# The last dispatch laid out anew, a third late place for weights, and w2 of three experts by columns

## The chip, the cores and the metric

The kernel runs on one core of a Trainium2 chip. A core has a matrix engine (TensorE; PE in the profile, its weight loads PEld), three engines for elementwise work (VectorE, ScalarE and GpSimd; DVE, ACT and POOL), a sync engine (SyncE, SP) from whose queue most transfers start, and 16 DMA engines between HBM and on-chip memory. The metric is the device time of one execution in microseconds (us). Before and after are compared by the median of their runs.

## The reference

```python
x = attention(rmsnorm(q) * g_q, rmsnorm(k) * g_k, v)   # 4 x 12 heads x 448 x 64 -> 1792 x 768
x = relu(x @ w_in) ** 2 @ w_out                        # 768 -> 2048 -> 768
logits = x @ phi                                       # 1792 x 32: 8 experts, 4 slots each
d = softmax(logits, axis=0);  slot_input = d.T @ x     # dispatch: over all 1792 tokens
h = relu(slot_input[e] @ w1[e]);  slot_out[e] = h @ w2[e]      # for each expert e
out = softmax(logits, axis=1) @ slot_out               # combine: over the 32 slots
```

The data are fp32. The weights w1 and w2 of the eight experts are 25 MB each.

## The kernel before, in words

One batch is 448 tokens and 12 heads. Attention goes through 24 pairs of heads. Beside it runs a filler (`Fill`), a list of generators: after a batch's last pair, `moe_hidden(b)` for that batch is appended, and attention gives it a turn according to costs written by hand (`PACE`, and the numbers that `yield` gives back). The last batch's `moe_hidden` runs when attention is over. The framework puts each engine's instructions into a fixed order when the program is built, by what it expects to be ready, and adds the semaphores; on the chip each engine follows its order.

`moe_hidden(b)` computes 16 blocks of 128 hidden units (`fc`): 18 matmuls (`ph`), relu on ScalarE, square on another engine (`gt`, 128 x 448). The hidden activations are not multiplied by w_out token by token. w_out @ phi is made beforehand (`wp`), so logits come straight from `gt`; and the dispatch sums `gt` over tokens first, and multiplies the 32 sums by w_out after. `group(g)`, for four blocks each: four matmuls give partial logits, one 32-row strip of a PSUM bank for each block, which VectorE adds to `lsb` (L567); then 16 transposes and four copies make `gn`, the same four blocks with tokens on partitions.

`dispatch(b)`: one matmul with `r4` adds the four strips of `lsb` and repeats the sum in each (L633); VectorE takes the maximum (`nmx`), ScalarE the exponential (`et`), four transposes and a copy give `en` (L656). For each group four matmuls weight `gn` by `en`, and VectorE adds the result to the running sums `gacc` (L664). At the end the combine softmax over slots is made from `lsb` (L668 to L680). After the last batch's dispatch, 16 matmuls with `i4s` add the strips of `gacc`, divide by the softmax sum and turn the result round (`gtt`, L821 to L825). Then `si_ps` = `gtt` times w_out (L850), then for each expert w1 (`pe`), relu into `hpad`, and w2 (`so_ps`); `finish` adds `so_ps`'s strips, splits the result in two parts (`stt`), multiplies by the combine weights `ct`, and sends the output.

[...] `si_ps` takes the two banks that `mps()` had.

Weights come in pieces of 128 x 1536 (768 KB) into 25 places (L795): 18 once attention's memory is free, two once the last `whl` tile is (`ring3`), five once `moe` is (`ring2`). The list `todo` fixes the order: 14 pieces of w_in, 8 of w_out (`wo`), 32 of w1, 32 of w2. A place is loaded again as soon as `done(key)` says that its piece was used, so each `fetch` on SyncE's queue waits for the matmuls of an older piece. For the last NL = 2 experts, w2 is cut by columns: two pieces hold three chunks each of columns 0 to 511 (2 KB runs in HBM), one has two full chunks, and a fourth has columns 512 to 767 of six chunks (1 KB runs). These fourth pieces come last of all, and `finish(0, 512)` doesn't need them:

```python
    for e in range(E):
        for x in range(3 if e >= E - NL else 4):
            expert_out(e, x)
    finish(0, CA)
    for e in range(E - NL, E):
        expert_out(e, 3)
    finish(CA, DM)
```

Of the kernel before, what the change touches and what calls it, by code (L numbers as in the profile page):

```python
# [47 lines left out]
def tile_attention_moe_softmoe(  # L48
# [49 lines left out]
    sel4 = const.tile([128, 2, 64], F32R, tag="sel4", name="sel4")  # L98
# [79 lines left out]

    xf = {}
# [363 lines left out]
    def moe_hidden(b):  # L543
# [12 lines left out]

        def group(g):
# [3 lines left out]
            ps = mps()  # L561
            for fi in range(4):
                mm(ps[32 * fi : 32 * fi + 32, :S], wp[:, 4 * g + fi, :], gt[fi])
            if g == 0:
                nc.vector.tensor_copy(lsb, ps[:, :S])
            else:
                nc.vector.tensor_tensor(lsb, lsb, ps[:, :S], ALU.add)  # L567
            yield 0.8
# [15 lines left out]
        pend = None  # L584
        for fc in range(NFC):
# [6 lines left out]
            for kc in range(KC):  # L592
# [3 lines left out]
                if kc % 3 == 2:  # L596
                    yield 1.7
            if n < LATE:
                w_load(n + 2)
            else:  # L600
                done(("wi", fc, 0))
# [18 lines left out]
            if b == B - 1:  # L620
                state["fc"] += 1
        for c in pend:
            yield c
# [3 lines left out]
        if b == B - 1:  # L627
            state["fc"] += 1
        yield from dispatch(b, lsb, gn)

    def dispatch(b, lsb, gn):
        ps = mps()
        mm(ps[:, :S], r4.rearrange("p j s -> p (j s)"), lsb)  # L633
# [3 lines left out]
        et = keep.tile([128, S], F32, tag="et", name=f"et_{b}", bufs=1)  # L637
        nc.vector.tensor_reduce(nmx, ps[:, :S], AX.X, ALU.max)
        if b > 0:
            nc.vector.tensor_tensor(nmx, nmx, m_run, ALU.max)  # L640
            nc.vector.tensor_tensor(al, m_run, nmx, ALU.subtract)
            nc.scalar.activation(al, al, AF.Exp)
        nc.vector.tensor_copy(m_run, nmx)
        nc.vector.tensor_scalar(nmx, nmx, -1.0, None, ALU.mult)
        nc.scalar.activation(et, ps[:, :S], AF.Exp, bias=nmx)
# [5 lines left out]
        yield 0.8  # L651
        ps = mps()
        for c in range(NC):
            nc.tensor.transpose(ps[:CP, c * NS : (c + 1) * NS], et[:NS, c * CP : (c + 1) * CP], ident[:NS, :NS])
        en = keep.tile([CP, NC, NS], F32, tag="en", name=f"en_{b}", bufs=1)
        nc.vector.tensor_copy(en, ps[:CP, : NC * NS].rearrange("p (c s) -> p c s", c=NC))  # L656
        yield 0.4
        for g in range(NG):
            ps = mps()
            for c in range(NC):  # L660
                mm(ps[32 * c : 32 * c + 32, :], en[:, c, :], gn[g][:, c, :])
            gs = gacc[g // 2][:, (g % 2) * 512 : (g % 2 + 1) * 512]
            if b > 0:
                nc.vector.scalar_tensor_tensor(gs, gs, al, ps, ALU.mult, ALU.add)  # L664
            else:
                nc.vector.tensor_copy(gs, ps)
            yield 0.9
        ps = mps()  # L668
        for c in range(NC):
            mm(ps[:CP, c * NS : (c + 1) * NS], lsb[:, c * CP : (c + 1) * CP], i4)  # L670
        pc = ps[:CP, : NC * NS].rearrange("p (c s) -> p c s", c=NC)
# [8 lines left out]
        nc.vector.tensor_tensor(cb, cb, cm[:, :, None].broadcast_to([CP, NC, NS]), ALU.mult)  # L680
        yield 0.8
# [48 lines left out]
    NL = 2  # L730
# [64 lines left out]
    SLOTS, SLOTS2, SLOTS3 = 18, 5, 2  # L795
# [15 lines left out]
    for _ in range(SLOTS2):  # L811
        fetch(ring2, SLOTS2)
    while fill.step() is not None:
        pass
    ex = tc.alloc_tile_pool(name="ex", bufs=1)
    srv = ex.tile([128, 1], F32, tag="srv", name="srv")
    nc.vector.tensor_scalar(srv, s_run, TINY, None, ALU.add)
    nc.vector.reciprocal(srv, srv)
# [202 lines left out]
```

## Time and profile before

| | |
|---|---|
| runs, median (lowest to highest) | 872.99 us (871.06 to 875.35) |
| profiled execution, its own time | 878.86 us |
| its span, first to last instruction | 877.10 us |
| TensorE busy | 755.5 us |
| VectorE, ScalarE, GpSimd busy | 557.8, 440.9, 133.9 us |
[...]
| bytes moved | 185.25 MB |

The rows below are from the profiled execution; their times count from its first instruction. A busy time is the union of an engine's instructions. One fp32 matmul stands as two records, so four matmuls are eight records.

### The profile page before, as it was taken

How to read it: one execution, taken by the hardware profiler on the slowest of the kernel's cores; microseconds unless marked ns; L12 is line 12 of the kernel's file. 1: busy time of each engine (PE TensorE's matmuls, PEld its weight loads, DVE VectorE, ACT ScalarE, POOL GpSimd, SP SyncE). 2: the span in 40 equal slices, each digit the busy share in tenths (PEclk: the TensorE clock that was granted, in tenths of full speed). 3: DMA queues.
4: the chain of work that ended last, by engine and by line, in shares of the span. 5: the costliest groups of instructions: out<-in, count | busy, mean ns of one | idle time of the engine just before them, and what ended most of it. 6: DMA issues, size and time to landing. Idle time of an engine off the chain costs nothing.

```text
span 877.1 us, 11761 instructions
## 1 busy us (share of the span) xinstructions
PE 755.5 (86%) x4040; PEld 532.6 (61%) x4040; DVE 557.8 (64%) x1030; ACT 440.9 (50%) x711; POOL 133.9 (15%) x132
## 2 busy tenths in 40 slices
PE   0497768879999999999999999999989998988563
PEld 0254445556678787768778766787877885534011
DVE  6795758888889786988777878866535123220013
ACT  2584746777778566746546665555442122010002
POOL 4140120220222121213122121211010000000000
PEclk9997877968999999999999999999999998799996
DMA  9795666787575554325435343433438996599978
GB/s 254 248 295 182 216 202 195 216 254 227 193 222 196 168 183 121 113 73 167 147 111 172 115 135 95 125 115 96 144 102 322 415 396 213 237 415 415 414 286 252
DMA packets 72988, 185.25 MB, mean 211 GB/s; under 512 B 17408, under 2 KB 41440, under 8 KB 72928
## 3 DMA queue, kind: packets, MB, share of 16 engines
q1 hardware_dynamic: 66736, 159.10, 52.6%
q0 software_dynamic: 5632, 25.17, 9.4%
q8 instruction: 32, 0.52, 0.3%
q10 hardware_dynamic: 560, 0.23, 0.1%
q14 instruction: 28, 0.23, 0.1%
HBM read 148.73 MB, written 24.38 MB: 197 GB/s over the span
## 4 chain that ended last, share of the span: by engine, by line
PE 64%; DMA 12%; DVE 11%; ACT 8%; issue 3%; SPq 1%; ACTq 0%; DVEq 0%
PE ph L138 25%; PE pss L138 11%; PE pv L138 10%; PE pm L138 7%; DMA w<-in_moe_w_dram 5%; PE pm L576 3%; DMA m<-m 3%; PE pe L138 3%; ACT p L338 2%; DMA wi_s<-wf 2%; ACT ph L342 2%; DVE pl L343 1%; DVE nm L316 1%; PE pt L138 1%; DVE wf L462 1%
## 5 line engine op out<-in xcount | busy, mean ns | idle before, releaser
L138 PE MATMUL ph<-xh,whl 128*128 128x448 f32 x900 | 217.4, 375 | 5.4 <-ACT gt L603 2.6
L138 PEld LDWEIGHTS ph<-xh,whl 128*128 128x128 f32 x900 | 165.5, 188 | 30.5 <-ACT gt L603 5.7
L138 PE MATMUL pss<-m,s 65*112 65x448 f32 (+1 forms) x384 | 119.3, 423 | 13.2 <-DMA m<-mt 7.5
L338 ACT ACTIVATE p<-pss 112x896 f32<-112x896 f32 x96 | 87.9, 917 | 49.9 <-PE pss L138 49.2
L316 DVE TENSOR_REDUCE nm<-pss 112x2 f32<-112x896 f32 x96 | 102.6, 1087 | 15.5 <-PE pss L138 14.2
L138 PEld LDWEIGHTS pss<-m,s 65*112 65x112 f32 (+1 forms) x384 | 72.5, 193 | 38.4 <-issue 18.5
L343 DVE TENSOR_TENSOR pl<-p,ph 112x896 fp32r<-112x896 f32 x62 | 71.4, 1153 | 31.7 <-ACT ph L342 31.4
L138 PE MATMUL pss<-s,m 128*112 128x448 f32 x192 | 62.5, 420 | 27.4 <-DMA m<-m 23.3
L138 PE MATMUL pv<-ph,vst 112*65 112x448 f32 (+1 forms) x272 | 82.5, 379 | 0.1
L252 POOL TENSOR_TENSOR qs<-qk,y 112x512 f32<-112x512 f32 x48 | 59.4, 1248 | 152.0 <-issue 58.0
L603 ACT ACTIVATE gt<-ph 128x448 f32<-128x448 f32 x64 | 34.8, 543 | 93.3 <-PE ph L138 86.2
L138 PE MATMUL pv<-p,vf 112*65 112x448 f32 x112 | 61.2, 661 | 5.6 <-ACT p L338 4.6
L611 POOL TENSOR_TENSOR gt<-gt 128x448 f32<-128x448 f32 x33 | 35.3, 1070 | 193.0 <-ACT gt L603 193.0
L342 ACT ACTIVATE ph<-pss 112x896 fp32r<-112x896 f32 x68 | 62.3, 916 | 0.1
L138 PEld LDWEIGHTS pss<-s,m 128*112 128x112 f32 x192 | 33.7, 191 | 46.5 <-issue 13.3
L138 PE MATMUL ph<-xh,wi 128*128 128x448 f32 x252 | 53.3, 367 | 0.0
L364 ACT COPY t<-pv 65x448 f32<-65x448 f32 x48 | 25.3, 527 | 53.9 <-PE pv L138 53.9
L138 PE MATMUL pv<-pl,vst 112*65 112x448 f32 x136 | 50.4, 370 | 1.8 <-DVE pl L343 1.8
L138 PEld LDWEIGHTS ph<-xh,wi 128*128 128x128 f32 x252 | 46.6, 188 | 3.4
L611 DVE TENSOR_TENSOR gt<-gt 128x448 f32<-128x448 f32 x22 | 13.7, 623 | 53.1 <-ACT gt L603 53.0
L138 PEld LDWEIGHTS pv<-ph,vst 112*65 112x65 f32 (+1 forms) x272 | 35.1, 136 | 16.9 <-ACT ph L342 1.9
L138 PE MATMUL so_ps<-w,hpad 128*32 128x512 f32 (+1 forms) x256 | 32.0, 493 | 15.4 <-DMA w<-in_moe_w_dram 15.4
(144 smaller groups left out, 1144.1 us busy)
## 6 DMA issues: line engine op xcount, KB each, us to landing
w<-in_moe_w_dram SPq DMA_DIRECT2D x62, 768.0 KB
whl<-wi_s SPq DMA_DIRECT2D x50, 768.0 KB
w<-in_moe_w_out_dram POOLq DMA_DIRECT2D x16, 768.0 KB, 5.6
w<-in_moe_w_in_dram POOLq DMA_DIRECT2D x16, 768.0 KB, 7.7
wi<-wi_s SPq DMA_DIRECT2D x14, 768.0 KB
wi_s<-wh SPq DMA_DIRECT2D x16, 384.0 KB
wi_s<-wf SPq DMA_DIRECT2D x16, 384.0 KB
wo_s<-wf SPq DMA_DIRECT2D x16, 384.0 KB
```

Of the source, the lines that this page charges most:

```text
L138: nc.tensor.matmul(o, lhsT, rhs, start=start, stop=stop)
L252: nc.gpsimd.tensor_tensor(x.rearrange("p c h d -> p h c d"), live[t]["qk"][i], y[:, 8 * i : 8 * i + 8] .rearrange("p (h c) -> p h c", h=2) ...
L316: nc.vector.tensor_reduce(nm[:, 2 * half : 2 * half + 2], ps[:CP, :, :S], AX.X, ALU.max, negate=True)
L338: nc.scalar.activation(p, ps[:CP, :, :S], AF.Exp)
L342: nc.scalar.activation(ph, ps[:CP, :, :S], AF.Exp)
L343: engine(ON_PL[t // NP * 4 + 2 * j + half]).tensor_tensor(pl, p, raw(ph), ALU.subtract)
L364: nc.scalar.copy(tt[: D + 1, j, :], ps[: D + 1, :S])
L462: nc.vector.scalar_tensor_tensor(fi, lo, 29, fi, ALU.logical_shift_right, ALU.bitwise_or)
L576: nc.tensor.transpose(ps[:CP, fi * 128 : (fi + 1) * 128], gt[fi][:, c * CP : (c + 1) * CP], ident)
L603: nc.scalar.activation(gt, ps[:, :S], AF.Relu)
L611: (nc.vector if k else nc.gpsimd).tensor_tensor(gt, gt, gt, ALU.mult)
```

## The change

In the last batch the partial logits of blocks 12 to 14 and the `r4` matmul are made inside block 15 (`partial`), the latter in a bank `lg` that stays open; block 15's logits are added into that bank by four matmuls, one for each strip. The maximum and the exponential (`peak`) read `lg` and come ahead of group 3's transposes. `et` overwrites `lsb`. In `dispatch_last` the `i4s` matmuls of a group follow the weighting of the next one, with a ScalarE copy for each group, and the combine softmax comes last, from transposes of `lg`. For the other batches, `et` becomes one of the six `gt` buffers. Everywhere the maximum is taken negated, and `en` is copied ahead of the sum over `et`. `ring3` has three places, and NL is 3, so w2 of experts 5 to 7 is cut by columns. `finish` subtracts the part that ScalarE wrote, so one VectorE copy is gone. `sel4`, `et` and `ch` move in memory.

```diff
-    sel4 = const.tile([128, 2, 64], F32R, tag="sel4", name="sel4")
...
+    sel4 = att.tile([128, 2, 64], F32R, tag="sel4", name="sel4")
...
+        last = b == B - 1
+        lg = []
+        def partial():
+            ps = mps()
+            for fi in range(3):
+                mm(ps[32 * fi : 32 * fi + 32, :S], wp[:, NFC - 4 + fi, :], gts[NFC - 4 + fi])
+            nc.vector.tensor_tensor(lsb[:96], lsb[:96], ps[:96, :S], ALU.add)
+            yield 0.8
+            lg.append(hps())
+            mm(lg[0][:, :S], r4.rearrange("p j s -> p (j s)"), lsb, True, False)
+            yield 0.8
...
         def group(g):
             gt = gts[4 * g : 4 * g + 4]
-            ps = mps()
-            for fi in range(4):
-                mm(ps[32 * fi : 32 * fi + 32, :S], wp[:, 4 * g + fi, :], gt[fi])
-            if g == 0:
-                nc.vector.tensor_copy(lsb, ps[:, :S])
+            if last and g == NG - 1:
+                for j in range(4):
+                    mm(lg[0][32 * j : 32 * j + 32, :S], wp[:, NFC - 1, :], gt[3], False, True)
+                yield 0.8
             else:
-                nc.vector.tensor_tensor(lsb, lsb, ps[:, :S], ALU.add)
-            yield 0.8
+                ps = mps()
+                for fi in range(4):
+                    mm(ps[32 * fi : 32 * fi + 32, :S], wp[:, 4 * g + fi, :], gt[fi])
+                if g == 0:
+                    nc.vector.tensor_copy(lsb, ps[:, :S])
+                else:
+                    nc.vector.tensor_tensor(lsb, lsb, ps[:, :S], ALU.add)
+                yield 0.8
...
+        first = partial()
         for fc in range(NFC):
...
                 if kc % 3 == 2:
                     yield 1.7
+                    if last and fc == NFC - 1:
+                        yield next(first)
...
+        if last:
+            yield next(pend)
+            nmx, al, sb = peak(b, lg[0], lsb)
         for c in pend:
             yield c
...
-        if b == B - 1:
+        if last:
             state["fc"] += 1
-        yield from dispatch(b, lsb, gn)
+            yield 0
+            yield from dispatch_last(lg[0], lsb, gn, al, sb)
+        else:
+            yield from dispatch(b, lsb, gn)
...
+    def peak(b, ps, et):
         nmx = keep.tile([128, 1], F32, tag="nmx", name=f"nmx_{b}", bufs=2)
         al = keep.tile([128, 1], F32, tag="al", name=f"al_{b}", bufs=2)
         sb = keep.tile([128, 1], F32, tag="sb", name=f"sb_{b}", bufs=2)
-        et = keep.tile([128, S], F32, tag="et", name=f"et_{b}", bufs=1)
-        nc.vector.tensor_reduce(nmx, ps[:, :S], AX.X, ALU.max)
+        nc.vector.tensor_reduce(nmx, ps[:, :S], AX.X, ALU.max, negate=True)
         if b > 0:
-            nc.vector.tensor_tensor(nmx, nmx, m_run, ALU.max)
-            nc.vector.tensor_tensor(al, m_run, nmx, ALU.subtract)
+            nc.vector.tensor_tensor(nmx, nmx, m_run, ALU.min)
+        nc.scalar.activation(et, ps[:, :S], AF.Exp, bias=nmx)
+        if b > 0:
+            nc.vector.tensor_tensor(al, nmx, m_run, ALU.subtract)
             nc.scalar.activation(al, al, AF.Exp)
         nc.vector.tensor_copy(m_run, nmx)
-        nc.vector.tensor_scalar(nmx, nmx, -1.0, None, ALU.mult)
-        nc.scalar.activation(et, ps[:, :S], AF.Exp, bias=nmx)
+        return nmx, al, sb
+
+    def slots(b, et, al, sb):
+        ps = mps()
+        for c in range(NC):
+            nc.tensor.transpose(ps[:CP, c * NS : (c + 1) * NS], et[:NS, c * CP : (c + 1) * CP], ident[:NS, :NS])
+        en = keep.tile([CP, NC, NS], F32, tag="en", name=f"en_{b}", bufs=1)
+        nc.vector.tensor_copy(en, ps[:CP, : NC * NS].rearrange("p (c s) -> p c s", c=NC))
         if b > 0:
             nc.vector.tensor_reduce(sb, et, AX.X, ALU.add)
             nc.vector.scalar_tensor_tensor(s_run, s_run, al, sb, ALU.mult, ALU.add)
         else:
             nc.vector.tensor_reduce(s_run, et, AX.X, ALU.add)
-        yield 0.8
-        ps = mps()
+        return en
+
+    def weighted(b, g, ps, en, gn, al):
         for c in range(NC):
-            nc.tensor.transpose(ps[:CP, c * NS : (c + 1) * NS], et[:NS, c * CP : (c + 1) * CP], ident[:NS, :NS])
-        en = keep.tile([CP, NC, NS], F32, tag="en", name=f"en_{b}", bufs=1)
-        nc.vector.tensor_copy(en, ps[:CP, : NC * NS].rearrange("p (c s) -> p c s", c=NC))
-        yield 0.4
-        for g in range(NG):
-            ps = mps()
-            for c in range(NC):
-                mm(ps[32 * c : 32 * c + 32, :], en[:, c, :], gn[g][:, c, :])
-            gs = gacc[g // 2][:, (g % 2) * 512 : (g % 2 + 1) * 512]
-            if b > 0:
-                nc.vector.scalar_tensor_tensor(gs, gs, al, ps, ALU.mult, ALU.add)
-            else:
-                nc.vector.tensor_copy(gs, ps)
-            yield 0.9
-        ps = mps()
-        for c in range(NC):
-            mm(ps[:CP, c * NS : (c + 1) * NS], lsb[:, c * CP : (c + 1) * CP], i4)
-        pc = ps[:CP, : NC * NS].rearrange("p (c s) -> p c s", c=NC)
+            mm(ps[32 * c : 32 * c + 32, :], en[:, c, :], gn[g][:, c, :])
+        gs = gacc[g // 2][:, (g % 2) * 512 : (g % 2 + 1) * 512]
+        if b > 0:
+            nc.vector.scalar_tensor_tensor(gs, gs, al, ps, ALU.mult, ALU.add)
+        else:
+            nc.vector.tensor_copy(gs, ps)
+
+    def combine_softmax(b, pc):
         cm = keep.tile([CP, NC], F32, tag="cm", name=f"cm_{b}", bufs=1)
         cb = cnat[:, b]
...
+    def dispatch(b, lsb, gn):
+        ps = mps()
+        mm(ps[:, :S], r4.rearrange("p j s -> p (j s)"), lsb)
+        et = moe.tile([128, S], F32, tag="gt", name=f"et_{b}", bufs=6)
+        nmx, al, sb = peak(b, ps, et)
+        yield 0.8
+        en = slots(b, et, al, sb)
+        yield 0.4
+        for g in range(NG):
+            weighted(b, g, mps(), en, gn, al)
+            yield 0.9
+        ps = mps()
+        for c in range(NC):
+            mm(ps[:CP, c * NS : (c + 1) * NS], lsb[:, c * CP : (c + 1) * CP], i4)
+        combine_softmax(b, ps[:CP, : NC * NS].rearrange("p (c s) -> p c s", c=NC))
+        yield 0.8
+
+    def dispatch_last(lg, et, gn, al, sb):
+        b = B - 1
+        en = slots(b, et, al, sb)
+        srv = state["ex"].tile([128, 1], F32, tag="srv", name="srv")
+        nc.vector.tensor_scalar(srv, s_run, TINY, None, ALU.add)
+        nc.vector.reciprocal(srv, srv)
+        i4s = state["ex"].tile([128, 32], F32, tag="i4s", name="i4s")
+        nc.vector.tensor_scalar(i4s, i4, srv, None, ALU.mult)
+        yield 0.4
+        gps = hps()
+        for g in range(NG + 1):
+            if g < NG:
+                weighted(b, g, mps(), en, gn, al)
+            if g > 0:
+                for fc in range(4 * g - 4, 4 * g):
+                    fo = fc % 8 * 128
+                    mm(gps[:, fc * NS : (fc + 1) * NS], gacc[fc // 8][:, fo : fo + 128], i4s)
+                f4 = slice(4 * g - 4, 4 * g)
+                nc.scalar.copy(gtt[:, f4], gps.rearrange("p (f s) -> p f s", s=NS)[:, f4])
+            yield 0.9
+        lgs = et[:NS]
+        nc.scalar.copy(lgs, lg[:NS, :S])
+        ps = mps()
+        for c in range(NC):
+            nc.tensor.transpose(ps[:CP, c * NS : (c + 1) * NS], lgs[:, c * CP : (c + 1) * CP], ident[:NS, :NS])
+        combine_softmax(b, ps[:CP, : NC * NS].rearrange("p (c s) -> p c s", c=NC))
...
-    NL = 2
+    NL = 3
...
-    SLOTS, SLOTS2, SLOTS3 = 18, 5, 2
+    SLOTS, SLOTS2, SLOTS3 = 18, 5, 3
...
     for _ in range(SLOTS2):
         fetch(ring2, SLOTS2)
+    ex = tc.alloc_tile_pool(name="ex", bufs=1)
+    state["ex"] = ex
     while fill.step() is not None:
         pass
-    ex = tc.alloc_tile_pool(name="ex", bufs=1)
-    srv = ex.tile([128, 1], F32, tag="srv", name="srv")
-    nc.vector.tensor_scalar(srv, s_run, TINY, None, ALU.add)
-    nc.vector.reciprocal(srv, srv)
-    i4s = ex.tile([128, 32], F32, tag="i4s", name="i4s")
-    nc.vector.tensor_scalar(i4s, i4, srv, None, ALU.mult)
-    ps = hps()
-    for fc in range(NFC):
-        fo = fc % 8 * 128
-        mm(ps[:, fc * NS : (fc + 1) * NS], gacc[fc // 8][:, fo : fo + 128], i4s)
-    nc.vector.tensor_copy(gtt, ps.rearrange("p (f s) -> p f s", s=NS))
...
-        ch = keep.tile([128, S], F32, tag="et", name=f"ch_{b}", bufs=1)
+        ch = keep.tile([128, S], F32, tag="lsb", name=f"ch_{b}", bufs=1)
...
         st = stt[:96, c0:c1]
-        sth = stt[:, DM + c0 : DM + c1]
         nc.vector.tensor_copy(sos, so_ps[:, c0:c1])
         ps = tps()
         mm(ps[:, :w], r4.rearrange("p j s -> p (j s)"), sos)
         nc.scalar.copy(st[0:64], ps[0:64, :w])
-        nc.vector.tensor_copy(sth[64:96], ps[64:96, :w])
-        nc.vector.tensor_tensor(st[64:96], ps[64:96, :w], raw(sth[64:96]), ALU.subtract)
+        nc.vector.tensor_tensor(st[64:96], ps[64:96, :w], raw(st[0:32]), ALU.subtract)
```

## Rows read from the trace of the kernel before

**Rows 1.** Stretches: length, busy us of each engine (xinstructions), PEclk, DMA share, GB/s.
```profile
672.00:720.00 48.00, 47.99 (x268) 41.64 (x264) 11.41 (x22) 10.27 (x20) 0.00 (x0) 1.00 1.02 415
720.00:739.20 19.20, 18.47 (x104) 13.88 (x96) 4.95 (x8) 5.31 (x10) 0.00 (x0) 1.00 0.56 184
749.60:758.40 8.80, 8.02 (x52) 6.15 (x55) 2.29 (x10) 0.71 (x3) 0.00 (x0) 0.59 0.01 5
758.40:847.00 88.60, 66.75 (x556) 24.40 (x548) 7.21 (x15) 5.90 (x19) 0.00 (x0) 0.98 1.02 407
847.00:850.30 3.30, 2.17 (x9) 0.77 (x10) 0.69 (x1) 0.00 (x0) 0.00 (x0) 1.00 0.87 279
850.30:855.60 5.30, 4.52 (x29) 1.75 (x30) 2.67 (x4) 1.74 (x4) 0.00 (x0) 1.00 0.02 6
855.60:874.50 18.90, 6.96 (x33) 4.20 (x29) 7.77 (x13) 5.75 (x11) 0.00 (x0) 0.72 0.97 290
```

**Rows 2.** The chain that ended last: start, length, work.
```profile
742.28 7.22 PE pm L138 x40
749.50 5.24 PE ph L138 x32
755.50 8.31 PE si_ps L138 x48
...
847.26 1.95 PE so_ps L138 x4
```

**Rows 3.** SyncE's queue, 745 to 765 us: what its issues waited for.
```profile
SPq L764 <- PE si_ps L138: 19.6, 6, 16.3
```

**Rows 4.** Timeline of TensorE from the last hidden block: start, length, work.
```profile
733.33 0.95 PE L138 MATMUL pm<-gt,wp 128*32 128x448 f32 x6
734.69 0.94 PE L138 MATMUL pm<-gt,wp 128*32 128x448 f32 x2
737.67 0.65 PE L576 MATMUL pm<-ident,gt 128*112 128x128 f32 x4 [0.24 <-ACT gn L148]
738.16 1.02 PE L138 MATMUL pm<-lsb,r 128*128 128x448 f32 x2
741.32 0.58 PE L654 MATMUL pm<-ident,et 32*112 32x32 f32 x4 [2.15 <-ACT et L645]
```

**Rows 5.** Timeline of VectorE and ScalarE, same stretch and just behind.
```profile
734.01 0.62 DVE L611 TENSOR_TENSOR gt<-gt 128x448 f32<-128x448 f32 x1 [2.97 <-ACT gt L603]
739.21 0.63 DVE L638 TENSOR_REDUCE nmx<-pm 128x1 f32<-128x448 f32 x1 [0.16 <-PE pm L138]
740.63 0.63 ACT L645 ACTIVATE et<-pm,nmx 128x448 f32<-128x448 f32 x1 [0.17 <-DVE nmx L644]
741.93 0.29 DVE L656 COPY en<-pm 112x128 f32<-112x128 f32 x1
749.88 0.28 DVE L675 TENSOR_TENSOR w<-pm,cm 112x128 f32<-112x128 f32 x1
```

**Rows 6.** Stretches of the dispatch, columns as in rows 1.
```profile
733.40:740.80 7.40, 5.07 (x26) 2.19 (x26) 3.19 (x8) 2.57 (x6) 0.00 (x0) 1.00 0.51 150
742.20:747.60 5.40, 5.32 (x28) 1.29 (x32) 2.20 (x7) 0.00 (x0) 1.81 (x1) 0.50 1.01 419
749.30:751.10 1.80, 1.80 (x19) 1.80 (x18) 0.75 (x4) 0.71 (x3) 0.00 (x0) 1.00 0.14 55
751.20:754.80 3.60, 3.52 (x17) 3.39 (x16) 0.04 (x1) 0.00 (x0) 0.00 (x0) 0.50 0.00 0
```

**Rows 7.** Stretches of the last weight transfers, columns as in rows 1.
```profile
825.50:831.50 6.00, 3.27 (x28) 0.58 (x32) 0.00 (x0) 0.00 (x0) 0.00 (x0) 1.00 1.02 417
832.50:845.00 12.50, 7.18 (x42) 1.32 (x42) 0.00 (x0) 0.00 (x0) 0.00 (x0) 1.00 1.04 390
846.50:849.00 2.50, 1.74 (x8) 0.50 (x8) 0.00 (x0) 0.00 (x0) 0.00 (x0) 1.00 1.09 345
```

**Rows 8.** Timeline of the step ahead of the output, VectorE.
```profile
851.81 0.69 DVE L957 CAST stt<-pt 32x512 fp32r<-32x512 f32 x1 [1.83 <-ACT stt L956]
```

More of the change, by code (lines that the diff above doesn't have):

```diff
@@ L626, in moe_hidden @@
                 convert_next()
-        if b == B - 1:
+        if last:
             state["fc"] += 1
-        yield from dispatch(b, lsb, gn)
-    def dispatch(b, lsb, gn):
-        ps = mps()
-        mm(ps[:, :S], r4.rearrange("p j s -> p (j s)"), lsb)
+            yield 0
[3 more added lines that the diff above has]
+    def peak(b, ps, et):
         nmx = keep.tile([128, 1], F32, tag="nmx", name=f"nmx_{b}", bufs=2)
@@ L650, in dispatch @@
             nc.vector.tensor_reduce(s_run, et, AX.X, ALU.add)
-        yield 0.8
-        ps = mps()
+        return en
+    def weighted(b, g, ps, en, gn, al):
         for c in range(NC):
-            nc.tensor.transpose(ps[:CP, c * NS : (c + 1) * NS], et[:NS, c * CP : (c + 1) * CP], ident[:NS, :NS])
-        en = keep.tile([CP, NC, NS], F32, tag="en", name=f"en_{b}", bufs=1)
-        nc.vector.tensor_copy(en, ps[:CP, : NC * NS].rearrange("p (c s) -> p c s", c=NC))
-        yield 0.4
-        for g in range(NG):
-            ps = mps()
-            for c in range(NC):
-                mm(ps[32 * c : 32 * c + 32, :], en[:, c, :], gn[g][:, c, :])
-            gs = gacc[g // 2][:, (g % 2) * 512 : (g % 2 + 1) * 512]
-            if b > 0:
-                nc.vector.scalar_tensor_tensor(gs, gs, al, ps, ALU.mult, ALU.add)
-            else:
-                nc.vector.tensor_copy(gs, ps)
-            yield 0.9
-        ps = mps()
-        for c in range(NC):
-            mm(ps[:CP, c * NS : (c + 1) * NS], lsb[:, c * CP : (c + 1) * CP], i4)
-        pc = ps[:CP, : NC * NS].rearrange("p (c s) -> p c s", c=NC)
+            mm(ps[32 * c : 32 * c + 32, :], en[:, c, :], gn[g][:, c, :])
[5 more added lines that the diff above has]
+    def combine_softmax(b, pc):
         cm = keep.tile([CP, NC], F32, tag="cm", name=f"cm_{b}", bufs=1)
```

## The prediction, made before the changed kernel was run

> **What bounds the kernel now.** I read the page's slices first: until about 660 us TensorE is nearly always busy and the transfers are moderate; from 870 us back to 760 us it is the other way round. So I asked for stretches from 672 us on. From 672 to 720 us TensorE is busy all the time and the DMA engines are full at 415 GB/s, filling the 25 places; from 720 us all places hold pieces and a transfer starts only when a block of w_in is done (share 0.56); from 749.6 to 758.4 us the DMA engines do nothing at all; then they are full for 88.6 us at 407 GB/s; then comes a second hole of 5.3 us; then the output, 18.9 us at 290 GB/s [rows 1]. Behind 758 us the end is set by bytes, and the order of the program only by the two holes.
>
> The first hole is named by SyncE's queue: its issue of a w1 piece waited 16.3 us for `si_ps` [rows 3]. All 25 places hold 8 pieces of w_out and 17 of w1, and none is free before the first w_out piece is used. That point is the end of a chain on TensorE [rows 2]: weighting from 742.28, `i4s` matmuls from 749.50, `si_ps` from 755.50; bytes flow 2.9 us later, at 758.4. So what starts `si_ps` earlier ends the kernel earlier, one for one, as long as the hole lasts. Ahead of it stands block 15, in a stretch where TensorE is always busy: what is moved into it delays it.
>
> The clock matters in this chain. [...]
>
> **The change, part by part.** *Lead-in of the dispatch.* Before, block 15 ends at 733.4; the square ends 1.2 us later, the fourth partial matmul follows at 734.69, and then `r4` is queued behind eight and four transposes and a copy until 738.16; maximum at 739.21, exponential at 740.63, `en` at 741.93, weighting at 742.28 [rows 2, 4, 5]. After: the partial matmuls and `r4` go into block 15 and delay its end by what they occupy, 0.95 and 1.02 us less their overlap [rows 4], I take 1.7: 735.1. With the same 1.3 us for relu and square, `lg` is completed from 736.4; four strips cost no more than one, since six records take 0.95 us and two take 0.94 [rows 4]: 737.35. Maximum 0.63, one short step instead of four (these lie between 739.84 and 740.63), exponential 0.63 [rows 5]: 738.9. The transposes of `et` (0.58) and `en` (0.29) would end at 739.8. But they need one of two banks, and group 3's transposes and copies go through the same two; three of the copies are on ScalarE, beside the exponential. Four ScalarE steps of about 0.63 from 737.5 end at 740.0, then 0.58, 0.29 and gaps give 741.0 for the weighting. Bounds: 739.9 without that wait, 742.3 if nothing is won. That is 1.3 us earlier.
>
> *Weighting and `i4s`.* The matmuls are the same 32 and 32 records, now mixed. At 0.50, 28 weighting records take 5.32 us, so 32 take 6.1; 17 `i4s` records take 3.52 us, so 32 take 6.6. At 1.00 the other 15 took about 1.8 us, so 32 take 3.8, and weighting half of 6.1, 3.05 [rows 6]. Before, the stage had some of each. Mixed, VectorE's sums are hidden behind the neighbouring group's matmuls, and three of four copies into `gtt` too; the eight combine records disappear from this place. But the combine softmax now stands between the last `i4s` and `si_ps`: `si_ps` takes the two `pm` banks, so it waits for the transposes of `lg` (0.58 as those of `et`), a maximum and a subtraction of about 0.28 each [rows 4, 5], 1.3 us with gaps, if they aren't drawn forward. At 0.50 throughout: 741.0 + 6.1 + 6.6 + 1.3 = 755.0, and 0.2 for waits on VectorE: 755.2, 0.3 us earlier than before. At 1.00 throughout: 741.0 + 3.05 + 3.8 + 1.3 = 749.2, 6.3 us earlier.
>
> Which one? Between block 15 and the weighting there is now `lg` (0.95 us), 16 transposes and the small ones of `et`; before, there were the partial matmuls, `r4` and the same transposes, and the clock fell at the end of it. I take 0.50, and since every wide group is now followed by 32-column matmuls, I don't expect it back before `si_ps`. [...]
>
> *A 26th place.* One piece more is loaded before the hole, from the stretch with share 0.56, where there is room. After the hole it is missing: 786 KB at 417 GB/s [rows 7] is 1.9 us. Zero only if the hole disappears, and it is 8.8 us long.
>
> *NL = 3.* The pieces after which `finish(0, 512)` can start are followed by three pieces instead of two. A piece of 1 KB runs goes at 345 GB/s, 2.28 us; of 2 KB runs at 390, 2.02; a plain one at 417, 1.89 [rows 7]. `finish` starts 2.28 us earlier against the last byte. Expert 5 pays 0.39 for its last piece and twice 0.13: 0.65 us. [...]
>
> *`finish`.* One copy of 0.69 us [rows 8] leaves the chain from the last `so_ps` (847.26, 1.95 us [rows 2]) to the first output at 855.6: 0.7 us less. With the above the second hole shrinks from 5.3 to 5.3 - 2.28 - 0.7 = 2.3 us, and the tail gains 2.28 + 0.7 - 0.65 = 2.35 us. Bounds: 3.0 if the runs cost nothing; 1.0 if late `so_ps` matmuls, waiting for their piece, stand in TensorE's order before the first output matmuls. The same copy in the second `finish` is hidden: output of the first 512 columns takes two thirds of 18.9 us.
>
> *The rest.* In the other three dispatches a short VectorE step disappears and `en` comes earlier; they run beside attention, where TensorE is the bound: nothing (bounds 0.5 us either way). `et` in a `gt` buffer: priced as a rival. Moved tiles: nothing.
>
> **The sum.** 0.3 + 1.9 + 2.35 = 4.55 us off the profiled execution's own 878.86 us (1.76 around its span of 877.10). That execution is 5.87 us above the median of the runs shown; I take the difference over to the median: 872.99 - 4.55 = 868.4 us. Part of the 5.87 can be clock that the runs had in this very stage, so that they have up to 1.5 us less to win; that is in the range.
>
> **Rivals.**
> 1. *The clock stays up.* `lg` and the transposes are closer together and the weighting starts earlier. Then the first term is 6.3 instead of 0.3: 862.4 us. For it: 1.00 held until 740.8 with TensorE a third idle. Against it: it fell in just such a stretch. Chance 0.25.
> 2. *The tail gives only its lower bound and the lead-in nothing*, because the order on TensorE or ScalarE puts a waiting instruction first: +1.0 instead of -0.3 in the first term, 1.9, 1.0: 871.1 us. For it: the orders are fixed before the run. Chance 0.16.
> 3. *Slower: `et` in the ring of six `gt` buffers.* If in the three batches beside attention the next batch's `gt` must wait for the last reader of `et`, block after block stalls in the stretch that TensorE bounds. To end slower than before by over 0.5% (4.4 us), the three places must cost 4.55 + 4.4, 3 us each: 877.4 us and more. Against it: a batch's `moe_hidden` begins only after the dispatch before, so `et` has been read when its buffer is wanted. Chance 0.04.
> 4. *As forecast, clock at 0.50*: 866 to 870 us. Chance 0.55.
>
> A measurement of this kernel can tell about 0.5% from no change, here 4.4 us: faster means below 868.6. The forecast lies just on this side; of its 0.55 I count 0.30 as faster. With rival 1: 0.55 faster, 0.41 the same, 0.04 slower. The range 861.5 to 871.7 us takes in rivals 1 and 2 and leaves out about 0.15.
>
> **What the profile after would show.** Block 15 ends near 735 and weighting starts near 741 (counted as before); if at 742.3, the two banks or ScalarE's order took the gain. The granted clock during weighting decides between 868 and 862. The hole before the w1 pieces is over near 758.1 (0.50) or 752 (1.00). The full stretch behind it has 46 pieces instead of 47, about 90.5 us to the last byte instead of 91.9. The second hole is near 2.3 us; at 3.5 or more rival 2 is right about the tail. Wrong would be all of it if attention ended at another time, or if the DMA engines no longer were full between the holes.

## The result, and the profile after

The changed kernel takes 862.51 us (median of 14 runs, 854.22 to 871.22), the kernel before beside it 875.38 us (14 runs, 870.39 to 884.15): a ratio of 0.984, 95% interval 0.980 to 0.988. Medians here and below are of all runs, ratios leave out the slow ones, over 1.5% above the fastest of the same kernel. By the medians it is faster by 12.9 us. The prediction had 4.55 us off; its range held the time, but the change is almost three times the one that was worked out.

The profiled execution took 860.87 us, its span 859.1 us, at a mean granted TensorE clock (PEclk; 1.00 is full speed) of 0.945, against 0.944 before. First its stretches, in the columns of [rows 1]:

```profile
727.70:733.30 5.60, 4.23 (x30) 2.15 (x28) 3.17 (x9) 3.15 (x7) 0.00 (x0) 1.00 0.54 151
733.30:741.50 8.20, 8.15 (x67) 4.74 (x68) 4.42 (x12) 0.90 (x4) 1.80 (x1) 1.00 0.97 388
741.60:744.90 3.30, 3.30 (x24) 1.40 (x27) 0.97 (x5) 0.86 (x4) 0.00 (x0) 0.50 0.57 217
745.00:834.50 89.50, 69.99 (x560) 25.78 (x553) 7.90 (x16) 6.12 (x20) 0.00 (x0) 0.96 1.02 402
834.50:838.30 3.80, 3.40 (x24) 1.27 (x18) 1.98 (x3) 1.91 (x4) 0.00 (x0) 1.00 0.24 76
```

The first line is the lead-in, from block 15's last matmul to the weighting; the second is the weighting and the `i4s` matmuls. The clock stays at 1.00 through both, where before it fell [rows 6]; it falls when `si_ps` starts. The first hole, 8.8 us with share 0.01 [rows 1], is now 3.3 us with 0.57, so 1.4 us are lost. The full stretch is 89.5 us long. Of the second hole 3.8 x 0.76 = 2.9 us are lost, against 5.3 x 0.98 and 3.3 x 0.13, together 5.6 us [rows 1].

The chain that ended last, from the same place as [rows 2]:

```profile
728.96 0.95 PE ph L137 x8
...
730.21 1.07 ACT gn L147 x2
731.28 0.54 ACT lsb L667
...
731.85 0.62 DVE sb L681
732.47 0.44 DVE gn L145
...
732.98 0.29 DVE en L679
...
733.32 1.92 PE pm L137 x16
...
735.25 1.08 PE ph L137 x8
...
740.70 1.24 PE ph L137 x8
741.94 6.83 PE si_ps L137 x48
```

The first `ph` is block 15's part of the logits, `lsb` the exponential, `sb` the sum over `et`, `pm` the weighting, and from 735.25 on `ph` is a group's `i4s` matmuls; `si_ps` follows the last of them at once. SyncE's longest wait for `si_ps`, 16.3 us in [rows 3], is 8.8:

```profile
SPq L833 <- PE si_ps L137: 10.6, 5, 8.8
```

TensorE, then VectorE and ScalarE, in the lead-in (as [rows 4, 5]):

```profile
724.71 0.95 PE L137 MATMUL pm<-gt,wp 128*32 128x448 f32 x6
...
727.50 0.91 PE L137 MATMUL ph<-lsb,r 128*128 128x448 f32 x2
...
728.96 0.96 PE L137 MATMUL ph<-gt,wp 128*32 128x448 f32 x8
732.44 0.40 PE L677 MATMUL pm<-ident,lsb 32*112 32x32 f32 x4 [0.45 <-ACT gn L147]
...
729.99 0.62 DVE L664 TENSOR_REDUCE nmx<-ph 128x1 f32<-128x448 f32 x1 [1.08 <-PE ph L137]
...
732.39 0.68 DVE L145 COPY gn<-pm 112x512 f32<-112x512 f32 x1
732.98 0.28 DVE L679 COPY en<-pm 112x128 f32<-112x128 f32 x1
...
730.21 1.07 ACT L147 COPY gn<-pm 112x512 f32<-112x512 f32 x2 [1.96 <-PE pm L595]
731.17 0.65 ACT L667 ACTIVATE lsb<-ph,nmx 128x448 f32<-128x448 f32 x1
```

Block 15 ends at 727.66. `r4` runs at 727.50, while relu and square are awaited. The maximum is at 729.99, but two copies into `gn` (1.07 us) stand ahead of the exponential, and on VectorE the sum over `et` (0.62 us) and another copy into `gn` stand ahead of `en`. The program names `en` ahead of the sum; in the order that was built, that holds only in the second dispatch, and in the other three the sum comes first.

**Three stages.** I cut every profile at three marks that all versions have: the maximum of the first dispatch, that of the third, and the first `si_ps` matmul.

| us | layout before | layout after | difference | forecast |
|---|---|---|---|---|
| first to third maximum, beside attention | 297.6 (297.5 to 297.7, four profiles) | 293.7 (293.6 to 293.8, seven) | -3.9 | 0 |
| third maximum to `si_ps` | 87.1 (86.9 to 87.3, three); before's own 90.0 | 82.9 (82.7 to 83.2, five) | -4.2; against before's own -6.8 | -0.3 |
| `si_ps` to the end | 121.8 (120.7 to 123.6, six) | 116.9 (116.0 to 117.8, five) | -4.9 | -4.25 |

The sum is -13.0 us, and the medians differ by 12.9; with before's own 90.0 in the second row it would be -15.9. Each row takes the profiles of this and the next section that have the layout of its column in that stage.

The second row leaves out, before, the two profiles with the exponential ahead in the last dispatch too (86.4 and 86.5), and after, those where `si_ps` starts among the `i4s` matmuls or `en` is made late; the last row leaves out those with `si_ps` among the `i4s` matmuls, and NL = 4.

Of the three old ones in the second row, two have the last dispatch in before's order (87.0 with new loads, 86.9 with `en` ahead of the sum in the program), and one has matmuls added (87.3). Before's own profile differs from the first two by the clock: it was at 0.50 from 741.0 to 747.7 us and again from 751.2, in the others for 3.4 us ahead of `si_ps`; weighting took 6.32 us for 5.34, and the `i4s` matmuls 5.39 for 3.74, together 2.6 us.

In two further profiles of the old order, 299.2 and 299.3 us in the first stage, the clock was at 0.50 for 3.4 us of it; at 1.00 all through it is 297.6.

### The profile page after: what moved, and what is told of

Same layout as the page of the kernel before. It is cut to its first block, busy times and chain, and to the rows that moved or that the text cites. A ratio compares the mean times of both kernels' runs of the same rounds, so it can differ in the third digit from the quotient of the medians.

```text
span 859.1 us, 11780 instructions
## 1 busy us (share of the span) xinstructions
PE 750.7 (87%) x4042; PEld 532.5 (62%) x4042; DVE 555.7 (65%) x1023; ACT 442.3 (51%) x716; POOL 136.3 (16%) x132
## 4 chain that ended last, share of the span: by engine, by line
PE 65%; DMA 11%; DVE 10%; ACT 8%; issue 4%; SPq 2%; ACTq 0%; POOL 0%; DVEq 0%
PE ph L137 25%; PE pv L137 12%; PE pss L137 11%; PE pm L137 6%; DMA w<-in_moe_w_dram 3%; PE pm L595 3%; PE pe L137 3%; DMA m<-m 3%; ACT p L338 2%; DVE pl L343 2%; DMA m<-mt 1%; ACT ph L342 1%; SPq L846 1%; PE pt L137 1%; PE pm L479 1%
## 5 line engine op out<-in xcount | busy, mean ns | idle before, releaser
L137 PE MATMUL pss<-m,s 65*112 65x448 f32 (+1 forms) x384 | 120.4, 425 | 13.3 <-DMA m<-mt 8.4
L252 POOL TENSOR_TENSOR qs<-qk,y 112x512 f32<-112x512 f32 x48 | 62.6, 1315 | 168.4 <-issue 76.3
L137 PE MATMUL pss<-s,m 128*112 128x448 f32 x192 | 59.8, 407 | 24.6 <-DMA m<-m 20.0
```

The lines of the kernel that those rows point to most:

```text
L137: nc.tensor.matmul(o, lhsT, rhs, start=start, stop=stop)
L252: nc.gpsimd.tensor_tensor(x.rearrange("p c h d -> p h c d"), live[t]["qk"][i], y[:, 8 * i : 8 * i + 8] .rearrange("p (h c) -> p h c", h=2) ...
```

## The experiments

My theory after this profile: three parts of like size. (1) Beside attention the short steps between maximum and `en` cost, because each waits behind long work on VectorE's queue and TensorE runs dry. (2) The last dispatch keeps the clock. (3) Loads and tail as forecast. The rivals: the clock is only held by the order of matmuls, or by chance; the buffer of `et` matters; there is one cause and not three.

**Only the maximum and exponential in the new order** (kernel before):

```diff
-        nc.vector.tensor_reduce(nmx, ps[:, :S], AX.X, ALU.max)
+        nc.vector.tensor_reduce(nmx, ps[:, :S], AX.X, ALU.max, negate=True)
         if b > 0:
-            nc.vector.tensor_tensor(nmx, nmx, m_run, ALU.max)
-            nc.vector.tensor_tensor(al, m_run, nmx, ALU.subtract)
+            nc.vector.tensor_tensor(nmx, nmx, m_run, ALU.min)
+        nc.scalar.activation(et, ps[:, :S], AF.Exp, bias=nmx)
+        if b > 0:
+            nc.vector.tensor_tensor(al, nmx, m_run, ALU.subtract)
             nc.scalar.activation(al, al, AF.Exp)
         nc.vector.tensor_copy(m_run, nmx)
-        nc.vector.tensor_scalar(nmx, nmx, -1.0, None, ALU.mult)
-        nc.scalar.activation(et, ps[:, :S], AF.Exp, bias=nmx)
```

> The kernel before, with only the new order of the short steps in all four dispatches (maximum taken negated, one comparison, then the exponential; the other steps behind it). Measured from the maximum of the first dispatch to the maximum of the third, it was 297.7 us before and 293.8 after the change. Theory queue (each short VectorE step that stood ahead of the exponential waited behind long VectorE work of attention, and TensorE ran dry): 293.8 within 0.6, and the median 3.5 to 5 us below before. Theory chance (the 3.9 us are a difference between two executions): 297.7 within 0.6 and a median within 2 us of before.

Measured: ratio 0.9965 [0.9927, 1.0003], medians 3.7 us apart; first to third maximum 295.5 us. About half of the stage's gain, between the two theories.

**Only `en` ahead of the sum** (kernel before):

```diff
-        if b > 0:
-            nc.vector.tensor_reduce(sb, et, AX.X, ALU.add)
-            nc.vector.scalar_tensor_tensor(s_run, s_run, al, sb, ALU.mult, ALU.add)
-        else:
-            nc.vector.tensor_reduce(s_run, et, AX.X, ALU.add)
...
         nc.vector.tensor_copy(en, ps[:CP, : NC * NS].rearrange("p (c s) -> p c s", c=NC))
+        if b > 0:
+            nc.vector.tensor_reduce(sb, et, AX.X, ALU.add)
+            nc.vector.scalar_tensor_tensor(s_run, s_run, al, sb, ALU.mult, ALU.add)
+        else:
+            nc.vector.tensor_reduce(s_run, et, AX.X, ALU.add)
```

> The kernel before, with one edit in every dispatch: en is copied ahead of the sum over et. First to third maximum took 297.7 to 299.3 us in the five profiles with the old order, 295.5 with only the steps ahead of the exponential put in the new order, 293.7 to 293.8 in four with all of it. Theory A (each short step on VectorE that stands in TensorE's way queues behind attention's long ones, and the two edits add up): 295.6 to 297, some 2 us less than with the old order. Theory B (the sum behind en costs nothing, and the whole gain beside attention comes from elsewhere, such as the buffer of et): 297.7 to 299.3 as before. The last dispatch: one VectorE step less ahead of the weighting, 8.3 to 9.0 us from block 15's end.

Measured: 0.9983 [0.9937, 1.0029]; 297.5 us. This edit alone gives 0.1 to 0.2 us, about what theory B said. In the second dispatch `en` starts 5.93 us behind the maximum, just as before: the framework again placed the sum ahead of it.

**Both orders** (kernel before, the two edits together, `et` where it was):

> The kernel before, with both edits to the order of the short steps in every dispatch (the exponential right behind the negated maximum, en ahead of the sum), et still in its own place in memory, all else as before. Theory A: first to third maximum 293.5 to 294.2 us as in the changed kernel, and some 4 us less time than the kernel before; with the weighting at about 8 us from block 15's end instead of 5.7. Theory B (the buffer of et is part of it): 295.5 as with the order ahead of the exponential alone, or more, and 2 us less time or no difference.

Measured: 0.9905 [0.9868, 0.9942], medians 7.8 us apart; 293.7 us. So the order makes the whole stage, and `et`'s buffer has no part in it. (The runs gained about twice what the stage did; why stays open.) The two edits are worth more together (3.9 us) than one by one (2.1 and 0.2). In the second dispatch `en` comes 3.27 us behind the maximum with the first alone and 3.08 with both; in the first dispatch 6.43 and 5.07, though the sum stands ahead of `en` in both. So the second edit also works by shifting the order that was built around it; how its 1.8 us come about isn't shown.

What the order does is seen best in the second dispatch. VectorE and then ScalarE of the kernel before, from the maximum to `en`:

```profile
523.59 0.62 DVE L638 TENSOR_REDUCE nmx<-pm 128x1 f32<-128x448 f32 x1 [0.27 <-PE pm L138]
524.13 1.08 DVE L343 TENSOR_TENSOR pl<-p,ph 112x896 fp32r<-112x896 f32 x1
525.13 0.15 DVE L640 TENSOR_TENSOR nmx<-nmx,m_run 128x1 f32<-128x1 f32 x1
525.20 1.08 DVE L316 TENSOR_REDUCE nm<-pss 112x2 f32<-112x896 f32 x1
526.20 0.15 DVE L641 TENSOR_TENSOR al<-m_run,nmx 128x1 f32<-128x1 f32 x1
526.27 1.08 DVE L316 TENSOR_REDUCE nm<-pss 112x2 f32<-112x896 f32 x1
527.27 0.14 DVE L643 COPY m_run<-nmx 128x1 f32<-128x1 f32 x1
527.33 0.62 DVE L552 TENSOR_TENSOR xh<-xf,xh 128x448 fp32r<-128x448 f32 x1
527.86 0.15 DVE L644 TENSOR_SCALAR nmx<-nmx 128x1 f32<-128x1 f32 x1
...
529.52 0.28 DVE L656 COPY en<-pm 112x128 f32<-112x128 f32 x1
...
528.04 0.64 ACT L645 ACTIVATE et<-pm,nmx 128x448 f32<-128x448 f32 x1 [0.78 <-DVE nmx L644]
```

Four steps of 0.15 us each stand behind a step of 0.62 to 1.08 us of attention or the next batch; so the exponential starts 4.45 us behind the maximum. In the changed kernel it has one step to wait for, and starts 1.72 us behind:

```profile
519.15 0.63 DVE L664 TENSOR_REDUCE nmx<-pm 128x1 f32<-128x448 f32 x1 [0.25 <-PE pm L137]
519.69 1.08 DVE L343 TENSOR_TENSOR pl<-p,ph 112x896 fp32r<-112x896 f32 x1
520.69 0.15 DVE L666 TENSOR_TENSOR nmx<-nmx,m_run 128x1 f32<-128x1 f32 x1
...
522.23 0.29 DVE L679 COPY en<-pm 112x128 f32<-112x128 f32 x1 [0.32 <-PE pm L677]
...
520.87 0.64 ACT L667 ACTIVATE et<-pm,nmx 128x448 f32<-128x448 f32 x1 [1.04 <-DVE nmx L666]
```

The stage from first to third maximum as one stretch, before and changed kernel:

```profile
367.78:665.52 297.74, 289.25 (x1555) 224.14 (x1556) 216.85 (x384) 165.54 (x271) 54.95 (x45) 1.00 0.39 123
```

```profile
364.92:658.70 293.78, 287.19 (x1555) 225.02 (x1556) 217.09 (x382) 165.26 (x270) 54.16 (x44) 1.00 0.40 124
```

TensorE does the same 1555 records. Its idle time falls from 8.49 to 6.59 us; the other 2.1 us lie in what counts as busy. Laid over each other, the two traces run level between the dispatches and shift in steps at them, by 1.6 us at the first and 2.4 us at the second.

That the order makes these 3.9 us is shown; that TensorE runs dry at the dispatches isn't. In the 23 us from 3 us ahead of the second maximum it is idle for 1.26 us before and 1.32 after. And at the first dispatch the exponential starts 3.44 us behind the maximum before and 0.70 after, but `en` 5.10 in both, so the 1.6 us there don't come from an earlier `en`. The path from the order to the time stays open.

**The changed kernel with the old order in these three dispatches** (`et` stays in the `gt` ring):

> The changed kernel, but the three dispatches beside attention have the old order of short steps again (the same number of them ahead of the exponential, the sum ahead of the copy of en). Theory queue: first to third maximum 297.7 within 0.6, median about 4 us above the changed kernel. Theory chance: 293.8 or anything between, median as the changed kernel.

Measured: 0.9869 [0.9816, 0.9922] against the kernel before; 297.6 us. The stage is back at its old length, also with `et` in the ring. The runs don't show the 4 us: the median is 861.1 us, not above the changed kernel's 862.5 and 863.8, and the intervals of the ratios overlap.

**Only loads and tail** (kernel before; `SLOTS3` = 3, `NL` = 3, `finish` without the copy, and the moved tiles, with `et` in the `gt` ring):

> The kernel before, with only what concerns transfers and the tail: the 26th place, w2 of three experts by columns, the shorter finish (and the tiles moved to make room). The prediction's terms: the stretch from the restart of the transfers to the last weight byte 1.3 us shorter (one piece less, 0.65 us of slower runs), the hole ahead of the output 2.3 instead of 5.3 us, 4.25 us off the median. Rival (late w2 matmuls stand ahead of the first output matmuls): hole of 3.5 or more, 3 us off. First to third maximum: 297.7, as nothing of the dispatch's order is changed.

Measured: 0.9960 [0.9924, 0.9996], some 3.5 us; the kernel ends 116.9 us behind the start of `si_ps`, as in the changed kernel. The second hole is 3.5 us with share 0.20, so 2.8 us are lost.

**Only the last dispatch** (the old-order version above, with 25 places, `NL` = 2 and the old `finish`; so the kernel before with `partial`, `lg`, `dispatch_last`, but with `et` in the `gt` ring and the moved tiles):

> The kernel before with only the last dispatch laid out anew (25 places, two experts by columns, old finish, old order in the other dispatches). From the end of block 15 to the first si_ps matmul it was 22.1 us before and 14.2 after. If the clock stays at 1.00 from block 15 to si_ps, as in the changed kernel's profile: about 14.2 and 6 to 7 us off the median. If it falls to 0.50 as the prediction had it: about 20 and 1 us or less off the median. First to third maximum 297.7.

Measured: 0.9992 [0.9956, 1.0029], medians 3.5 us apart; third maximum to `si_ps` 82.7 us, and `si_ps` 14.05 us behind block 15, with the clock at 1.00. Its profile shows the whole 4.2 us, its runs hardly, and not the 6 to 7 us expected (the interval ends at 0.44% faster, 3.8 us). But the old-order version above, which is this one with the loads, has a ratio of 0.9869 where the loads alone have 0.9960, some 8 us less. Six to twelve runs that spread over 12 to 19 us don't settle such parts; I go by the stages, and why the runs of this kernel gained less than its stage stays open.

**The `i4s` matmuls behind all of the weighting again** (changed kernel):

```diff
-        for g in range(NG + 1):
-            if g < NG:
-                weighted(b, g, mps(), en, gn, al)
+        for g in range(NG):
+            weighted(b, g, mps(), en, gn, al)
+        for g in range(1, NG + 1):
```

> The changed kernel with the weighting of all four groups first and the i4s matmuls behind it. In three executions with the new layout the clock held 1.00 from block 15 up to si_ps, and 14.1 us passed between the end of block 15 and si_ps. Theory lead-in (it holds because the lead-in is shorter and fuller): the clock is 1.00 into the i4s matmuls here too, which may lose it near their end; 14 to 15.5 us. Theory mix (the wide weighting between the narrow i4s matmuls holds it): the clock falls within the i4s matmuls and si_ps starts at 0.50, 15.5 us or more.

Measured: 0.9824 [0.9773, 0.9875]. The clock is at 1.00 all through, and `si_ps` starts 13.3 us behind block 15:

```profile
726.50:732.10 5.60, 4.23 (x30) 2.15 (x29) 3.17 (x9) 3.14 (x7) 0.00 (x0) 1.00 0.50 149
732.20:735.90 3.70, 3.69 (x32) 0.66 (x32) 2.76 (x6) 0.00 (x0) 1.80 (x1) 1.00 0.91 361
735.90:739.70 3.80, 3.42 (x32) 3.15 (x28) 1.84 (x7) 0.93 (x4) 0.00 (x0) 1.00 1.01 422
```

So it isn't the mixing that keeps the clock. The weighting takes 3.86 us at 1.00, 3.69 of them in the second line.

**The old layout with matmuls in its gaps** (kernel before; before and behind `r4` of the last batch six records into a spare bank that nothing reads):

> The kernel before with three more matmuls in its last dispatch, whose result nobody reads: 448 columns each, beside the maximum and the exponential, where TensorE stood idle for 2.15 us. Theory lead-in: the clock does not fall before the weighting (1.00 until the i4s matmuls at least), weighting takes 4.0 us instead of 6.3, and si_ps starts 2 us or more earlier after block 15 than the 22.1, 18.9 and 19.5 us seen with the old layout. Rival (the clock falls all the same, the transposes ahead are enough): weighting at 0.50, 20 to 23 us.

Measured: 0.9973 [0.9943, 1.0004]. The weighting is as late as before (9.0 us behind block 15), but runs at 1.00, in 3.86 us; the clock falls later, among the `i4s` matmuls, and `si_ps` starts 19.5 us behind block 15, against 22.1 in before's own profile, but no earlier than the 18.9 to 19.5 us of the other four with the old layout. So its clock theory held, and its gain didn't:

```profile
730.70:739.60 8.90, 7.36 (x36) 3.52 (x33) 4.04 (x11) 3.02 (x6) 0.00 (x0) 1.00 0.57 182
739.70:744.30 4.60, 4.58 (x41) 1.46 (x41) 3.55 (x7) 0.00 (x0) 1.80 (x1) 1.00 1.02 421
746.50:750.10 3.60, 2.84 (x14) 2.70 (x13) 0.73 (x2) 0.00 (x0) 0.00 (x0) 0.50 0.14 60
```

**The new layout with `en` late** (changed kernel; six ScalarE copies of `et` onto itself stand ahead of its transposes):

> The changed kernel with six ScalarE copies of et onto itself ahead of its transposes, so that TensorE waits about 3.8 us longer before the weighting. Prices the clock: it should fall to 0.50 before the weighting. If narrow and wide matmuls mixed do not bring it back, as the prediction had it, weighting and i4s take 12.5 to 13 us instead of 8.5 and si_ps starts 7 to 8 us later after block 15 than in the changed kernel (14.1 us); if the clock comes back among them, 9.5 to 11.5 us and si_ps 5 to 6.5 us later.

Measured: 0.9954 [0.9915, 0.9993]; weighting 9.2 and `si_ps` 19.4 us behind block 15.

```profile
731.10:737.20 6.10, 3.80 (x26) 1.85 (x24) 2.41 (x6) 4.08 (x9) 0.00 (x0) 1.00 0.54 152
737.30:740.10 2.80, 0.58 (x4) 0.44 (x4) 0.85 (x3) 1.97 (x5) 0.00 (x0) 0.50 0.97 393
740.20:744.10 3.90, 3.88 (x18) 0.91 (x18) 1.57 (x6) 0.27 (x1) 1.80 (x1) 0.50 1.01 421
744.20:750.30 6.10, 6.08 (x52) 4.17 (x51) 2.79 (x7) 0.80 (x3) 0.00 (x0) 1.00 0.37 153
```

With a lead-in as long as the old one (9.2 us for 8.9) and emptier (TensorE busy 3.80 of 6.10 us, before 5.07 of 7.40 [rows 6]) the clock falls before the weighting, also in the new layout. And it comes back at 744.2, among mixed wide and narrow matmuls: the second half of my step on the clock was wrong as well. Lateness and clock together take 5.2 us. From the third maximum to `si_ps` it is 88.7 us, against 82.9 in the new layout and 87.1 in the old: more than the whole layout had given.

**A bank of its own for the transposes of `et`, and NL = 4** (changed kernel):

> The changed kernel with a PSUM bank of its own for the last transposes of et (they waited for a copy of group 3), and four experts by columns. If the terms of the tail hold: from block 15 to the weighting 5.1 instead of 5.66 us; the second hole 2.3 us less again, nearly closed, 0.65 us more of slower runs: 1.5 to 2 us off the changed kernel, which is little more than its measurement can tell. Rival (late w2 matmuls in TensorE's order ahead of the first output matmuls): the hole stays 2 us or more and nothing is gained.

Measured: 0.9819 [0.9778, 0.9860]. Weighting at 5.74 us, not earlier. The transposes did wait for the bank: they start 4.25 us behind block 15 instead of 4.77. But `en` comes no earlier (5.31 for 5.32), as the sum and a copy into `gn` stand ahead of it on VectorE. The second hole is 3.0 us with share 0.36, so 1.9 us are lost where it was to be nearly closed; that is nearer to the rival's 2 us. `si_ps` to the end 116.0 instead of 116.9 us, which is within the spread.

**The changed kernel again, and a combination** (NL = 4, own bank, `i4s` behind the weighting, one copy of group 3 from ScalarE to VectorE):

> The changed kernel again, to stand beside the others of this call. All theories: first to third maximum 293.8, block 15's end to the weighting 5.66 and to si_ps 14.1 to 14.2, end behind the start of si_ps 117 us, ratio to the kernel before 0.98 to 0.988. If the clock falls ahead of the weighting this time, then that it held in five profiles was chance, and si_ps comes at 16 us or later.

> The changed kernel with what looked useful: w2 of four experts by columns (117.2 to 116.0 us behind the start of si_ps), the i4s matmuls behind the whole weighting again (clock 1.00 all through, si_ps 0.8 us earlier), a PSUM bank of its own for the transposes of et, and one of group 3's copies taken from ScalarE to VectorE, so that the exponential comes earlier. Theory A (a ScalarE copy of 1.07 us stands ahead of the exponential): weighting 4.6 to 5.2 us from block 15's end instead of 5.66, si_ps at 12.3 to 13, and 2 to 3 us less time than the changed kernel. Rival: VectorE, which then has two copies ahead of en, takes what ScalarE gives: weighting at 5.6 to 5.8, and 1 to 2 us less.

Measured: 0.9844 [0.9788, 0.9899] and 0.9820 [0.9749, 0.9892], medians 863.8 and 863.3 us: no difference that can be told. In the combination the weighting comes at 5.89 us and `si_ps` at 13.6, outside theory A and nearer to the rival's number, though for another reason. ScalarE of the combination:

```profile
725.27 0.58 ACT L147 COPY gn<-pm 112x512 f32<-112x512 f32 x1 [1.96 <-PE pm L595]
726.60 0.58 ACT L147 COPY gn<-pm 112x512 f32<-112x512 f32 x1 [0.74 <-PE pm L595]
727.08 0.64 ACT L667 ACTIVATE lsb<-ph,nmx 128x448 f32<-128x448 f32 x1
```

The order still has a copy of group 3 ahead of the exponential, and that one now waits 0.74 us for its transposes. None of my versions beats the changed kernel by more than can be measured.

## Why the prediction was off, point by point

- *"The rest: nothing (bounds 0.5 us either way)".* This failed first: it is 3.9 us. The reason given, that TensorE is the bound there, is true of its sum (busy 289.25 of 297.74 us), and the stage still got shorter when only the order of short steps changed. VectorE is busy 216.85 of 297.74 us, and in the second dispatch four short steps of 0.14 to 0.15 us on its queue each start only at about the end of a step of 0.62 to 1.08 us that stands ahead. I had given the order no price at all, and not asked what is queued ahead of each step; how much of the 3.9 us is that wait isn't shown.
- *"I take 0.50 ... I don't expect it back before `si_ps`".* This failed second, and is of like size: I had 14.2 us from the weighting to `si_ps` (741.0 to 755.2), measured are 8.6 (733.32 to 741.9). In all seven profiles with the new last dispatch and `en` not delayed, the clock was at 1.00 from block 15 to within 0.5 us of `si_ps`. What TensorE did ahead of the weighting: busy 4.23 of 5.60 us, and the clock held; 7.36 of 8.90, and it held; 5.07 of 7.40 [rows 6], and it fell; 3.80 of 6.10 with `en` late, and it fell. In the kernel before, it fell while TensorE stood idle for 2.15 us ahead of the transposes of `et` [rows 4]. Length alone doesn't decide it, since the second of these held for 8.90 us; whether the shorter lead-in of the new layout would do without being fuller I haven't told apart. I had carried the fall over from the old lead-in, as the new one has the same 16 transposes and the small ones; the clock holds all the same. And I had taken the 32-column matmuls behind every wide group as a reason for the clock to stay at 0.50 until `si_ps`. In the old layout it fell to 0.50 among the `i4s` matmuls (751.2 us [rows 6]), but no run shows that these are the cause. In the mixed stretch, where they follow the wide ones group by group, TensorE is busy 8.15 of 8.20 us and the clock is at 1.00; with `en` late it comes back to 1.00 among them, at 744.2 us.
- *Rival 1* had the clock right and gave 862.4 us, almost the measured time, partly by chance. Its first term of 6.3 us is 6.8 in the profiled pair; but before's own execution was 2.9 us late in this stage (90.0 for 87.1), and against the other executions it is 4.2. Half of 6.1, 3.05 us, for the weighting at 1.00 was too low: it takes 3.86. It had 10.55 us off 872.99; measured are 12.9 off 875.38, 3.9 of them from beside attention, which no rival had.
- *Lead-in 5.9 us:* 5.66. The size is right, the reason in part: group 3's copies on ScalarE stand ahead of the exponential, as named. The wait for one of the two banks was there too, but what lasted longest behind the exponential was VectorE, with the sum and a copy into `gn` ahead of `en`, which I hadn't named.
- *`partial` and `r4` delay block 15's end by 1.7 us:* 1.2 (third maximum to block 15's end 67.6 before, 68.8 after, means of six and eight profiles). `r4` runs in the wait for relu and square (727.50 to 728.41 us, block 15's part of the logits follows at 728.96), so one set counts and not two.
- *The combine softmax, 1.3 us ahead of `si_ps`:* 0.4 us, its four transposes; they were drawn forward, between the last two groups of `i4s`, and the rest of it delays nothing.
- *Loads and tail, 4.25 us:* 4.9. Right. The second hole loses 2.9 us where I had 2.3, and 2.7 us less than before where I had 3.0; the full stretch is 89.5 us where I had 90.5. My sign for rival 2, a hole of 3.5 us or more, was badly put: the hole is 3.8 us long, but with share 0.24, and the stage gained all the same.
- *`et` in the `gt` ring, slower:* costs nothing.

## What to carry to other kernels

In the second dispatch here, steps of 0.14 to 0.15 us on VectorE, which is busy 216.85 of the stage's 297.74 us, started only at about the end of the step of 0.62 to 1.08 us ahead of them on the queue. Where a chain hops from TensorE over such a queue and back, count the hops, and take out those that the next engine need not wait for; that TensorE is the bound of the whole stretch is no reason to price this at nothing: here it was 3.9 us. Look at the order that was built, too: one of the two edits changed nothing by itself. And read a stage's price from several executions where there are some: the one profile of before was 2.9 us late in the very stage under study.

## What was not expected of the hardware

Up to the first maximum TensorE has the same order of work in all 14 profiles, and yet 13 of them reach it between 360.6 and 368.0 us, and one at 371.7. The granted clock differs: between 60 and 240 us it goes to and fro between 1.00 and 0.50, in other places each time, and it is at 0.50 for 61.4 us of the stretch in the earliest profile and for 65 to 79 us in the others. That isn't all of it: of five profiles with 75 us at 0.50 the earliest reaches the mark at 364.1 and the latest at 371.7. One stretch of the kernel before, and of the combination:

```profile
180.00:240.00 60.00, 55.15 (x232) 37.85 (x232) 51.34 (x98) 45.10 (x68) 12.34 (x11) 0.82 0.70 220
```

```profile
180.00:240.00 60.00, 55.88 (x246) 39.30 (x247) 52.40 (x93) 46.35 (x70) 12.34 (x12) 0.88 0.64 207
```

TensorE gets through 232 records in it at a mean clock of 0.82, and through 246 at 0.88. These differences of 7 us and more between profiles are about half of what runs of one kernel spread over (17 us for the changed kernel), and that is why stages, not medians, had to tell the parts apart.
